# Sparse attention with a gated feed-forward layer: the first 512 keys loaded in 32 by 32 blocks and transposed by VectorE

## Chip, cores and metric

The kernel runs on one core of a Trainium2 chip. The metric is the device time of one execution in microseconds. Before the change it is 560.16 us, the median of 3 runs (559.36 to 561.0).

The engines are named as the profile names them: PE is TensorE, PEld its loading of weights, DVE is VectorE, ACT is ScalarE, POOL is GpSimd, SP is SyncE. A name with q, as SPq, is the engine's queue of issued work.

## The reference

For each of 8 batches and 8 heads, 576 queries attend to 576 keys of 64 numbers. Only scores within `tau` of the row's maximum count. The heads are joined, and a feed-forward layer with a gate follows.

```python
scores = scale * np.matmul(q, k.transpose(0, 1, 3, 2))
thresh = np.max(scores, axis=-1, keepdims=True) - tau
scores = np.where(scores >= thresh, scores, -1000000000.0)
scores = scores - np.max(scores, axis=-1, keepdims=True)
attn = np.exp(scores)
attn = attn / (np.sum(attn, axis=-1, keepdims=True) + 1e-09)
attn_out = np.matmul(attn, v)                       # (8, 8, 576, 64), float32
x = attn_out.transpose(0, 2, 1, 3).reshape(4608, 512)
h = x @ w_in                                        # (4608, 2048)
g = h * np.clip(h + 3.0, 0.0, 6.0) / 6.0
out = g @ w_out                                     # (4608, 512)
```

## The kernel before

Two heads are a pair, two pairs a quad; there are 16 quads, two to a batch. A quad is worked in 9 slots: slots 0 to 3 are 128 queries each of its first pair, slots 4 to 7 those of its second, and slot 8 the last 64 queries of all four heads. Each slot also does a piece of the feed-forward layer of an earlier batch: a first-layer item (`mm1`, with `mm1_relu` and `mm1_gate`), except in slot 8, and mostly one part of a second-layer tile (`mm2_part`).

The scores need queries and keys with the 64 head numbers on partitions, the two heads of a pair in the two halves. So both have to be transposed after loading. Batches 0 and 1 (`b < NB`, `NB = 2`) do this with TensorE for both. From batch 2 on queries come as 32 by 32 blocks, and VectorE transposes each block; keys are still transposed by TensorE and copied out of PSUM. The values are laid out so that key number `4 p + t` lies on partition `p`, and the keys are transposed in that order.

```python
def main(dst, src, h, order, by=nc.sync):
    by.dma_start(out=dst[:, :, h, :], in_=src[b, 4 * g + h, 0:512, :].rearrange(order, t=4))

def blocks_q(n, a, j):                       # queries, from the third batch on
    c = 32 * (2 * a + j)
    nc.sync.dma_start(out=nq[c:c + 32, n * S:(n + 1) * S].rearrange("p (k d) -> p k d", d=32),
                      in_=q[b, 4 * g + 2 * n + a, :, 32 * j:32 * j + 32].rearrange("(k r) d -> r k d", r=32))

# ...
for n in range(2):                           # five loading jobs to a quad, one started per slot
    loads.append(lambda n=n: [main(km, k, 2 * n + a, "(p t) d -> p t d") for a in range(2)])
    loads.append(lambda n=n: load_q(n))
    if n == 0:
        loads.append(rest)                   # keys 512 to 575 (and those queries, for b < NB)

# ...
def by_pe(pair):
    return pair // NPAIR < NB

def main_pe(src, pair):
    ps = bank("tp")
    n = pair % 2
    for t in range(4):
        nc.tensor.transpose(ps[:, t * P:(t + 1) * P], src[:, t, 2 * n:2 * n + 2, :], identf[:])
    return ps

def transpose_q(pair):
    nq = nat[pair // 2][0]
    if by_pe(pair):
        ps = main_pe(nq[:, 0:1024].rearrange("p (t h d) -> p t h d", h=4, t=4), pair)
        return lambda: nc.vector.tensor_copy(out=qT_of(pair)[:, 0:512], in_=ps[:])
    n = pair % 2
    nc.vector.transpose(out=qT_of(pair), in_=nq[:, n * S:(n + 1) * S])

def transpose_k(pair):
    ps = main_pe(nat[pair // 2][1], pair)
    return lambda: copy_out(kT_of(pair)[:, 64:576], ps[:])    # ScalarE from slot number 22 on
```

The loop over the slots, cut to the order of work in one slot:

```python
for n, sl in enumerate(queue):
    # ...
    if slot == (4 if quad else 8) and quad + 2 < NQUAD:
        load_quad(quad + 2)                  # appends the five jobs
    # ...
    if prev is not None:
        for i in range(2):
            sm_exp(prev, i)                  # ScalarE
    sm_max(sl)                               # VectorE row maximum, GpSimd bias
    if slot != 8 and todo1:
        item, then = todo1.pop(0)
        h = mm1(item)                        # TensorE, one PSUM buffer
        r = mm1_relu(h, on_act=(slot in (0, 1, 3, 5)))   # ScalarE, or else VectorE
        mm1_gate(item, h, r)                 # VectorE
        todo2.extend(then)
    # ...                                    # reciprocal (VectorE), second-layer parts (TensorE)
    for i in range(2):
        sm_mask(sl, i)                       # ScalarE
    evict = None
    nxt = 2 * quad + 2
    if slot == (1 if quad else 2):
        evict = transpose_q(2 * quad + 1)
    elif slot == (2 if quad else 3):
        evict = transpose_k(2 * quad + 1)
    # ...
    elif slot in (5, 6, 7) and quad + 1 < NQUAD:
        if slot == 5:
            alloc_qk(quad + 1)
            evict = transpose_q(nxt)
        elif slot == 6:
            evict = transpose_k(nxt)
        else:
            evict = transpose_rest(quad + 1)
    # ...                                    # attention times values in slots 3, 4 and 8
    if evict:
        evict()
    # ...
    if n + 1 < len(queue):
        queue[n + 1].tiles = scores(queue[n + 1].quad, queue[n + 1].slot)   # TensorE
    # ...
    if prev is not None:
        sm_norm(prev)                        # GpSimd, then mostly a transposing transfer (SyncE)
    flush()                                  # outputs
    late.extend(outs)
    start(loads, 1)                          # one loading job
```

Of the kernel before, what the change touches and what calls it, by code (L numbers as in the profile page):

```python
# [21 lines left out]
def kernel(  # L22
# [10 lines left out]
    nc = tc.nc  # L33
# [8 lines left out]
    NB = 2  # L42
# [25 lines left out]
    nat = {}  # L68
# [5 lines left out]
    loads = []  # L74
# [5 lines left out]
    def load_quad(quad):  # L80
        b, g = divmod(quad, 2)
        nat[quad] = (nat_pool.tile([P, 1152], F32, tag="nq", name="nq"),
                     nat_pool.tile([P, 4, 4, D], F32, tag="km", name="km"),
                     nat_pool.tile([P, 2 * D], F32, tag="kr", name="kr"))
        nq, km, kr = nat[quad]

        def main(dst, src, h, order, by=nc.sync):
            by.dma_start(out=dst[:, :, h, :], in_=src[b, 4 * g + h, 0:512, :].rearrange(order, t=4))

        def blocks_q(n, a, j):  # L90
            c = 32 * (2 * a + j)
            nc.sync.dma_start(out=nq[c:c + 32, n * S:(n + 1) * S].rearrange("p (k d) -> p k d", d=32),
                              in_=q[b, 4 * g + 2 * n + a, :, 32 * j:32 * j + 32].rearrange("(k r) d -> r k d", r=32))

        def load_q(n):
            if b < NB:
                for a in range(2):
                    main(nq[:, 0:1024].rearrange("p (t h d) -> p t h d", h=4, t=4), q, 2 * n + a, "(t p) d -> p t d",
                         by=nc.scalar if quad == n == 0 else nc.sync)
            else:  # L100
                for a in range(2):
                    for j in range(2):
                        blocks_q(n, a, j)

        def rest():
            for dst, src in ((kr[:], k), (nq[:, 1024:1152], q))[0:2 if b < NB else 1]:
                for n in range(2):
                    nc.sync.dma_start(out=dst[64 * n:64 * n + 64, :].rearrange("p (h d) -> p h d", h=2),
                                      in_=src[b, 4 * g + 2 * n:4 * g + 2 * n + 2, 512:S, :].rearrange("h p d -> p h d"))

        for n in range(2):
            loads.append(lambda n=n: [main(km, k, 2 * n + a, "(p t) d -> p t d") for a in range(2)])
            loads.append(lambda n=n: load_q(n))
            if n == 0:
                loads.append(rest)

    def load_v(b):
        vm = v_pool.tile([P, H, 4 * D], BF16, tag="vm", name="vm")
        vr = vrs[b % 2]
        vsb[b] = (vm, vr)  # L120
        for g in range(2):
            vcasts.append(lambda g=g: nc.gpsimd.dma_start(
                out=vm[:, g * 4:g * 4 + 4, :],
                in_=v[b, g * 4:g * 4 + 4, 0:512, :].rearrange("h (p t) d -> p h (t d)", t=4)))
        for a in range(2):
            vcasts.append(lambda a=a: nc.gpsimd.dma_start(
                out=vr[a * 64:(a + 1) * 64, a, :, :],
                in_=v[b, :, 512:S, :].rearrange("(hp a) p d -> a p hp d", a=2)[a]))
# [57 lines left out]
    def kT_of(pair):  # L186
        return qkT[pair // 2][1][:, pair % 2, :]
# [4 lines left out]
    def bank(name):  # L192
        nonlocal turn
        turn += 1
        if now < N2 and turn % 2:
            return ps_o.tile([P, 512], F32, tag="o", name=name)
        return ps_m.tile([P, 512], F32, tag="m", name=name)


    def copy_out(out, in_):  # L200
        if 0 <= now < N1:
            nc.vector.tensor_copy(out=out, in_=in_)
        else:
            nc.scalar.copy(out=out, in_=in_)  # L204
# [11 lines that stand above are left out]
# [7 lines left out]
        nc.vector.transpose(out=qT_of(pair), in_=nq[:, n * S:(n + 1) * S])  # L223

    def transpose_k(pair):
        ps = main_pe(nat[pair // 2][1], pair)
        return lambda: copy_out(kT_of(pair)[:, 64:576], ps[:])

# [63 lines left out]
    def sm_exp(sl, i):  # L292
        s = sl.s[:, i, :]
        nc.scalar.activation(out=s, in_=s, func=Act.Exp, accum_out=sl.rsum[:, i:i + 1])  # L294
# [67 lines left out]
    def mm1_relu(hps, on_act):  # L362
        w = hps.shape[2]
        r = r_pool.tile([P, 2, 320], F32, tag="r", name="r")[:, :, 0:w]
        if on_act:
            nc.scalar.activation(out=r, in_=hps, func=Act.Relu, bias=three[:])  # L366
        else:
            nc.vector.tensor_scalar(out=r, in0=hps, scalar1=3.0, scalar2=0.0, op0=Alu.add, op1=Alu.max)  # L368
        return r

    def mm1_gate(item, hps, r):
        b, ni, c0, w = item
        c0 += (b % 2) * S
        nc.vector.scalar_tensor_tensor(out=gbuf[:, ni:ni + 2, c0:c0 + w], in0=r, scalar=6.0, in1=hps,  # L374
                                       op0=Alu.min, op1=Alu.mult)
# [63 lines left out]
    for n, sl in enumerate(queue):  # L439
        quad, slot = sl.quad, sl.slot  # L440
        b, g = divmod(quad, 2)
        now = n
        if slot in (0, 4):
            pts[2 * quad + slot // 4] = pt_pool.tile([P, 9, 512], BF16, tag="pT", name="pT")
        if slot == 8:
            ptr[quad] = ptr_pool.tile([P, 9, P], BF16, tag="pR", name="pR")
        if quad == 0 and slot == 0:
            load_quad(1)
        if slot == (4 if quad else 8) and quad + 2 < NQUAD:
            load_quad(quad + 2)  # L450
        if slot == 0 and g == 1 and b + 1 < B:
            load_v(b + 1)
        if prev is not None:
            for i in range(2):
                sm_exp(prev, i)
        sm_max(sl)

        if slot != 8 and todo1:
            item, then = todo1.pop(0)
            h = mm1(item)  # L460
            r = mm1_relu(h, on_act=(slot in (0, 1, 3, 5)))
            mm1_gate(item, h, r)
            todo2.extend(then)
        copies = pe_transpose(queue[n - 2]) if n > 1 and queue[n - 2].on_chip else None
        if prev is not None:
            sm_recip(prev)
        if copies:
            copies()
        outs = []


        pieces = 0 if slot == 3 else 1
        if slot == 0:
            second = True
        if second and slot < 2 and len(todo2) > 1 and todo2[0][1] == todo2[1][1]:
            pieces, second = 2, False
        for _ in range(pieces):
            if todo2:
                bb, mt, part = todo2.pop(0)
                mm2_part(bb, mt, part)  # L480
                if part == 3:
                    outs += mm2_out(bb, mt, on_act=False)
        for i in range(2):
            sm_mask(sl, i)
# [6 lines that stand above are left out]
        elif n == 1:  # L491
            evict = transpose_rest(0, of_k=False)
        elif slot == 3 and quad > 0:
            av_main(2 * quad - 1)
        elif slot == 4 and quad > 0:
            av_rest(quad - 1)
            if quad % 2 == 0:
                todo1.extend(moe_of(quad // 2 - 1))
# [8 lines that stand above are left out]
        elif slot == 8:  # L507
            av_main(2 * quad)
# [3 lines that stand above are left out]
            warm_up(8)  # L512
        if n + 1 < len(queue):
            queue[n + 1].tiles = scores(queue[n + 1].quad, queue[n + 1].slot)
        if n < 8:
            warm_up(6)
        if prev is not None:
            sm_norm(prev)
        flush()
        late.extend(outs)  # L520
        start(loads, 1)
        if n < 4 or n > 12:
            start(vcasts, 1)
        if n > 3:
            start(casts, 1 if n < 24 else 2)
        prev = sl
# [80 lines left out]
```

## Time and profile before

| what | before |
|---|---|
| time, median of 3 runs | 560.16 us |
| span of the profiled run | 558.7 us |
| key transposes on TensorE (`tp<-identf,km`) | 128 matmuls, 273 ns each in the mean |
| copies of 512 transposed keys, ScalarE | 27, 563 ns in the median |
| query transposes on VectorE (128x576) | 24, 758 ns in the median |
| transfers for 512 keys of one head | 64, 128 KB each, 3.0 us to landing |
| transfers for queries in blocks | 96, 72 KB each, 2.7 us to landing |
| packets of all transfers | 286348 |

A busy time says how long an engine had an instruction in hand. The chain is the work that ended last, followed back from the end, at each step to what released it. A long busy time off this chain costs nothing by itself. Matmuls overlap, so that the duration of one is longer than what the next one has to wait.

### The profile page before, as it was taken

The numbers are of one execution on the slowest core, as the hardware profiler recorded it, in microseconds if no ns is written. First come the engines' busy times: TensorE is split into PE (matmuls) and PEld (weight loads), VectorE is DVE, ScalarE is ACT, GpSimd is POOL, SyncE is SP. The second block draws the span as 40 slices with busy tenths as digits, with TensorE's granted clock in tenths as the row PEclk, the third lists the DMA queues.
The fourth block names the chain that finished last, engine by engine and source line by source line (L and its number), as shares of the span: only waits on it lengthen the run. The fifth ranks groups of instructions, "written<-read, shape, count | busy, mean of one in ns | idle before, by whom it ended". The sixth has DMA issues, their size and how long they took to land.

```text
span 558.7 us, 11624 instructions
## 1 busy us (share of the span) xinstructions
PE 530.6 (95%) x3829; PEld 309.2 (55%) x3870; DVE 424.7 (76%) x1041; ACT 469.7 (84%) x999; POOL 305.3 (55%) x646
## 2 busy tenths in 40 slices
PE   8899798799999999999999999999999999999997
PEld 6655455555555555655555555655555565654663
DVE  3787686787878788887978788887978798883440
ACT  4899899798889999899898999899898999984440
POOL 2788878854556555755556555755556555561000
PEclk9999899999999999999999999999999999999999
DMA  5999979976789869978689889977689865454102
GB/s 121 137 120 173 196 128 190 204 142 126 137 158 152 152 136 157 178 149 146 130 148 152 173 131 160 175 147 147 131 145 166 150 144 114 100 109 94 38 20 76
DMA packets 286348, 77.52 MB, mean 139 GB/s; under 512 B 269264, under 2 KB 281808, under 8 KB 286288
## 3 DMA queue, kind: packets, MB, share of 16 engines
q1 hardware_dynamic: 267680, 67.47, 65.3%
q0 software_dynamic: 17408, 8.92, 13.6%
q8 instruction: 30, 0.49, 0.4%
q10 hardware_dynamic: 1200, 0.39, 0.3%
q14 instruction: 30, 0.25, 0.1%
HBM read 36.70 MB, written 9.44 MB: 83 GB/s over the span
## 4 chain that ended last, share of the span: by engine, by line
PE 55%; DVE 11%; ACT 8%; issue 4%; SPq 3%; DMA 2%; POOL 2%; DVEq 0%; POOLq 0%
PE h L357 17%; PE o L386 16%; PE s L260 15%; DVE s L281 5%; PE av L327 3%; ACT s L289 3%; ACT s L294 3%; DMA nq<-in_q_dram 2%; DVE g L374 2%; DVE r L368 2%; ACT r L366 1%; PE s L266 1%; PE tp L214 1%; SPq L310 1%; POOL pn L302 1%
## 5 line engine op out<-in xcount | busy, mean ns | idle before, releaser
L302 POOL TENSOR_SCALAR pn<-s,rinv 128x576 bf16<-128x576 f32 x288 | 211.6, 745 | 133.1 <-DVE rinv L297 57.3
L289 ACT ACTIVATE s<-s,bias 128x576 f32<-128x576 f32 x288 | 206.9, 766 | 36.3 <-POOL bias L284 35.2
L281 DVE TENSOR_SCALAR_CACHE_REDUCE s<-s 128x576 f32<-128x576 f32 x288 | 205.9, 752 | 40.3 <-PE s L260 29.9
L294 ACT ACTIVATE s<-s 128x576 f32<-128x576 f32 x288 | 192.7, 671 | 0.3
L260 PE MATMUL s<-kT,qT 64*128 64x288 f32 x1024 | 169.7, 430 | 5.1 <-DVE s L281 2.8
L357 PE MATMUL h<-xT,w_in_sb 128*128 128x320 bf16 (+1 forms) x1024 | 144.9, 287 | 5.9 <-DVE g L374 5.0
L386 PE MATMUL o<-w_out_sb,g 128*128 128x512 bf16 x535 | 133.5, 379 | 5.2 <-DVE osb L394 3.0
L357 PEld LDWEIGHTS <-w_in_sb 128*128 128x128 bf16 x1024 | 92.1, 97 | 68.9 <-issue 31.9
L374 DVE SCALAR_TENSOR_TENSOR g<-r,h 128x512 bf16<-128x512 f32 (+1 forms) x128 | 96.4, 755 | 41.7 <-ACT r L366 39.9
L260 PEld LDWEIGHTS s<-kT,qT 64*128 64x128 f32 x1024 | 93.7, 186 | 60.9 <-DVE s L281 24.0
L284 POOL TENSOR_SCALAR bias<-m 128x1 f32<-128x1 f32 x288 | 54.4, 189 | 66.6 <-DVE s L281 45.8
L386 PEld LDWEIGHTS <-g 128*128 128x128 bf16 x576 | 55.6, 98 | 57.4 <-issue 9.0
L366 ACT ACTIVATE r<-h,three 128x640 f32<-128x640 f32 (+1 forms) x74 | 54.4, 736 | 20.6 <-PE h L357 19.9
L294 ACT ACTIVATION_READ_ACCUMULATOR s<-s 128x1 f32 x288 | 54.2, 188 | 0.0
L368 DVE TENSOR_SCALAR r<-h 128x512 f32<-128x512 f32 (+1 forms) x54 | 40.5, 751 | 0.0
L394 DVE TENSOR_SCALAR osb<-o 128x512 f32<-128x512 f32 x31 | 21.0, 676 | 21.4 <-PE o L386 21.4
L327 PE MATMUL av<-pT,vm 128*64 128x512 bf16 x256 | 34.6, 393 | 2.0 <-ACT kT L204 2.0
L327 PEld LDWEIGHTS <-vm 128*64 128x64 bf16 x512 | 18.0, 111 | 25.3 <-issue 18.8
L297 DVE RECIPROCAL rinv<-rsum 128x2 f32<-128x2 f32 x144 | 23.0, 160 | 11.3 <-ACT s L294 10.5
L339 DVE CAST xT<-av 128x512 bf16<-128x512 f32 x32 | 21.8, 681 | 6.6 <-PE av L330 6.3
L281 DVE DVE_READ_ACCUMULATOR s<-s 128x1 f32 x288 | 23.9, 83 | 0.0
L266 PE MATMUL s<-kT,qT 64*64 64x288 f32 x256 | 20.1, 415 | 0.7 <-DVE s L281 0.7
(44 smaller groups left out, 241.4 us busy)
## 6 DMA issues: line engine op xcount, KB each, us to landing
km<-in_k_dram SPq DMA_DIRECT2D x64, 128.0 KB, 3.0
out_dram<-osb SPq DMA_DIRECT2D x31, 256.0 KB, 2.4
nq<-in_q_dram SPq DMA_DIRECT2D x96, 72.0 KB, 2.7
vm<-in_v_dram POOLq DMA_DIRECT2D x16, 256.0 KB, 5.6
w_in_sb<-in_moe_w_in_dram POOLq DMA_DIRECT2D x16, 128.0 KB, 4.3
w_out_sb<-in_moe_w_out_dram POOLq DMA_DIRECT2D x16, 128.0 KB, 4.5
pT<-pn SPq DMA_TRANSPOSE x119, 3.4
nq<-in_q_dram SPq DMA_DIRECT2D x14, 128.0 KB, 4.4
```

What stands on the lines that cost most here:

```text
L260: nc.tensor.matmul(tiles[a][:, hf, 0:HALF], qT_of(pair)[a * 64:(a + 1) * 64, t * P:(t + 1) * P], keys(pair, a, hf), start=True, stop=True)
L281: nc.vector.tensor_scalar(out=sl.s[:, i, :].rearrange("p (a b) -> p a b", a=2), in0=ps[:, :, 0:HALF], scalar1=1.0, scalar2=None, op0=Alu.m ...
L284: nc.gpsimd.tensor_scalar(out=sl.bias[:, i:i + 1], in0=sl.m[:, i:i + 1], scalar1=-scale, scalar2=tau, op0=Alu.mult, op1=Alu.add)
L289: nc.scalar.activation(out=s, in_=s, func=Act.Prelu, bias=sl.bias[:, i:i + 1], scale=scale, alpha=REJECT)
L294: nc.scalar.activation(out=s, in_=s, func=Act.Exp, accum_out=sl.rsum[:, i:i + 1])
L302: nc.gpsimd.tensor_scalar(out=pn[:, i, :], in0=sl.s[:, i, :], scalar1=sl.rinv[:, i:i + 1], scalar2=1.0, op0=Alu.mult, op1=Alu.mult)
L327: nc.tensor.matmul(ps[a * 64:(a + 1) * 64, :], vm[:, 2 * hp + a, c * D:(c + 1) * D], pT[:, 5 * a + c, cols], start=(c == 0), stop=False)
L357: nc.tensor.matmul(hps[:, n, 0:w], w_in_sb[:, ki, (ni + n) * P:(ni + n + 1) * P], xT[b][:, ki, c0:c0 + w], start=(ki == 0), stop=(ki == KI ...
L366: nc.scalar.activation(out=r, in_=hps, func=Act.Relu, bias=three[:])
L368: nc.vector.tensor_scalar(out=r, in0=hps, scalar1=3.0, scalar2=0.0, op0=Alu.add, op1=Alu.max)
L374: nc.vector.scalar_tensor_tensor(out=gbuf[:, ni:ni + 2, c0:c0 + w], in0=r, scalar=6.0, in1=hps, op0=Alu.min, op1=Alu.mult)
L386: nc.tensor.matmul(o_ps[0], gbuf[:, ni, mt * P:(mt + 1) * P], w_out_sb[:, ni, :], start=(ni == 0), stop=(ni == NI - 1))
```

## The change

From the third batch on (`b >= NB`) the first 512 keys of each head are loaded like the queries: four transfers to a pair, each filling 32 partitions with 32 by 32 blocks, two halves of the head numbers for each of two heads. Within the blocks the keys stand in the order of the values, so that VectorE's transposition of each block puts them where TensorE's transposes and the copy had put them. TensorE then needs no key transposes and ScalarE no copy for these pairs. As VectorE has one more instruction for each pair and ScalarE one less, one first-layer ReLU per quad goes from VectorE to ScalarE from quad 4 on: ScalarE does it in slots 1, 2, 3, 5 and 6 instead of 0, 1, 3 and 5. The last 64 keys are treated as before.

```diff
+        def blocks_k(n, a, j):
+            c = 32 * (2 * a + j)
+            nc.sync.dma_start(
+                out=km[c:c + 32].rearrange("p t h d -> p (t h d)")[:, n * 512:(n + 1) * 512].rearrange(
+                    "p (t m d) -> p t m d", t=4, d=32),
+                in_=k[b, 4 * g + 2 * n + a, 0:512, 32 * j:32 * j + 32].rearrange("(m r t) d -> r t m d", r=32, t=4))
+
+        def load_k(n):
+            if b < NB:
+                for a in range(2):
+                    main(km, k, 2 * n + a, "(p t) d -> p t d")
+            else:
+                for a in range(2):
+                    for j in range(2):
+                        blocks_k(n, a, j)
...
-            loads.append(lambda n=n: [main(km, k, 2 * n + a, "(p t) d -> p t d") for a in range(2)])
+            loads.append(lambda n=n: load_k(n))
...
     def transpose_k(pair):
+        if not by_pe(pair):
+            n = pair % 2
+            km = nat[pair // 2][1][:].rearrange("p t h d -> p (t h d)")
+            nc.vector.transpose(out=kT_of(pair)[:, 64:576], in_=km[:, n * 512:(n + 1) * 512])
+            return None
         ps = main_pe(nat[pair // 2][1], pair)
         return lambda: copy_out(kT_of(pair)[:, 64:576], ps[:])
...
-            r = mm1_relu(h, on_act=(slot in (0, 1, 3, 5)))
+            r = mm1_relu(h, on_act=(slot in ((1, 2, 3, 5, 6) if quad >= 2 * NB else (0, 1, 3, 5))))
```

## The prediction

> **What bounds the kernel now.** I read the page's first two parts, then the busy time in three stretches, then the chain that ended last, then the groups of the stretch that matters.
>
> ```profile
> PE 530.6 (95%) x3829; PEld 309.2 (55%) x3870; DVE 424.7 (76%) x1041; ACT 469.7 (84%) x999; POOL 305.3 (55%) x646
> ```
>
> TensorE is busy nearly throughout, ScalarE next. That is an average, so the same count by stretch, the first ending where the steady part begins:
>
> ```profile
> core 0: us, PE busy (x) PEld busy (x) DVE busy (x) ACT busy (x) POOL busy (x), PEclk, DMA share, GB/s
> 115.00:145.00 30.00, 28.85 (x208) 16.09 (x209) 24.85 (x61) 26.99 (x60) 15.78 (x34) 1.00 0.72 138
> 145.00:505.00 360.00, 353.19 (x2582) 202.49 (x2615) 298.83 (x735) 328.91 (x709) 204.68 (x434) 1.00 0.82 145
> 505.00:559.00 54.00, 48.43 (x303) 27.57 (x305) 19.90 (x28) 17.51 (x25) 0.98 (x2) 0.99 0.18 53
> ```
>
> In the steady 360 us TensorE has 6.8 us free, ScalarE 31.1 (91% busy), VectorE 61.2 (83%), and the DMA engines are busy 82%. A ceiling follows: if TensorE sets the pace, work taken from it is the only thing worth much, and ScalarE is next at 9%. But the chain through the same stretch is not TensorE alone:
>
> ```profile
> by line: PE s L260 20.9%; PE h L357 19.4%; PE o L386 16.7%; DVE s L281 5.3%; issue 4.6%; PE av L327 4.4%; DMA nq<-in_q_dram 3.1%; ACT s L289 2.8%; ACT s L294 2.7%; DVE g L374 2.3%; DVE r L368 2.1%; PE s L266 1.9%; PE tp L214 1.6%; SPq L310
> ```
>
> The key transposes are 1.6% of 360 us here, 5.8 us. Each set of four is a 0.44 us step of the chain, so about 13 of the 22 sets of this stretch (88 matmuls) lie on it. Where they don't, the chain runs through ScalarE, as in this piece of it (start, duration, what):
>
> ```profile
> 212.51 1.27 issue
> 213.78 1.47 POOL pn L302 x2
> 215.25 0.08 issue
> 215.34 0.20 POOL bias L284
> 215.54 0.02 issue
> 215.56 1.44 ACT s L289 x2
> 217.00 0.15 ACT kT L204
> ```
>
> There the softmax loop GpSimd, ScalarE, VectorE was last, and the key copy on ScalarE was part of it.
>
> **What the skill says.** The Trainium skill, "VectorE: DVE Perf Modes", § The three transpose paths: VectorE transposes 32 by 32 blocks only, SBUF to SBUF, where TensorE does the full 128 by 128 and lands in PSUM; hence the new load order. It gives 311 ns against 390 ns for 128x128 bf16. The trace has the float32 case: VectorE takes 758 ns for 128x576 queries (row below); TensorE takes 0.44 us for four 128x128 tiles plus 563 ns of ScalarE for the copy out. The skill, "DMA: Bandwidth & Descriptors", § Why small descriptors are slow (HBM only): a fixed overhead of about 3 cycles per packet on top of size/32. From it I estimate 7 cycles for 128 bytes against 11 for 256, so halving packets costs 14/11, 27% more. The trace's packet records have a median of 13 ns for 128 bytes and 18 ns for 256: two for one cost 44% more. The measurement counts. The skill, "Perfetto Trace Analysis", § Identifying the Most-Contended Engine, warns that matmul busy time overstates TensorE; the trace agrees so far that its chain gives PE only 55% of the span against 95% busy. I therefore treat the 6.8 us of free time as too small, and the full saving as a ceiling.
>
> **The change part by part.**
>
> ```profile
> L223 DVE STREAM_TRANSPOSE qT<-nq 128x576 f32<-128x576 f32 x22 | 16.7, 760 | 0.0
> L368 DVE TENSOR_SCALAR r<-h 128x512 f32<-128x512 f32 x24 | 16.5, 686 | 0.0
> L366 ACT ACTIVATE r<-h,three 128x640 f32<-128x640 f32 x23 | 18.0, 786 | 6.2 <-PE h L357 6.1
> L366 ACT ACTIVATE r<-h,three 128x512 f32<-128x512 f32 x24 | 16.3, 680 | 3.6 <-PE h L357 3.5
> L214 PE MATMUL tp<-identf,km 128*128 128x128 f32 x88 | 13.2, 273 | 0.0
> L204 ACT COPY kT<-tp 128x512 f32<-128x512 f32 x22 | 12.4, 563 | 0.0
> ```
>
> (busy us, then mean ns, in these groups of 145 to 505 us.) The tile's own list has 24 such copies, from 118.0 to 482.4 us, which are the 24 pairs of quads 4 to 15; so everything below counts 24.
>
> TensorE loses 24 sets of four, 0.44 us each as chain steps: 10.6 us. By the busy column, 13.2/22 = 0.60 us a set, 14.4 us; but a modelled end overlaps the next matmul, so 0.44 is the right unit.
>
> ScalarE loses 24 copies. One is 563 ns alone, but its neighbours start 0.47 us apart (the chain's "ACT kT L204" steps), so 11.3 us. It takes over one ReLU in each of 12 quads: five of eight slots in place of four. By the busy column (18.0+16.3)/47 = 0.73 us, 8.8 us. Net about -2.5 us.
>
> VectorE gains 24 transposes of 128x512. Scaled from 760 ns for 576 elements (a start every 0.68 us in its timeline, so 0.61 for 512): 14.6 us. It gives up 12 ReLUs at (18.0+16.5)/46 = 0.75 us: 9.0 us. Net +5.6 us, against 61.2 us free.
>
> The DMA engines: per pair 1024 packets of 256 bytes become 2048 of 128. With the mean packet times of the records (22.9 and 13.7 ns), 1024 x 22.9 / 16 = 1.47 us becomes 2048 x 13.7 / 16 = 1.75 us, +0.3 us a pair, +7 us in all spread over some 380 us: the 82% becomes about 84%. SyncE's queue issues four loads a pair for two. Two now cost 2 x 0.627 = 1.25 us (their median); four query block loads of nearly the same shape cost 4 x 0.497 = 1.99. So +0.7 us a pair, 18 us of issuing in all, in the slots 4 and 7 of each quad, beside transposing transfers of 1.3 us each. In five consecutive slots (4 to 8) of some 3.5 us, SyncE then issues 5 x 1.3 (transposes) + 8 x 0.5 (keys) + 8 x 0.5 (queries) + 1.3 (rest) + about 1.5 (outputs) = 17.3 us of 17.5. That is full, where before it was 15.8.
>
> Slot by slot, ScalarE does 1.34 us of exponentials and 1.44 of masks everywhere, 2.8 us. Slots 2 and 6 had a copy (0.47) and now have a ReLU (0.73), slot 0 loses its ReLU. So in slots 1 to 3 and 5 to 7, where a pair's keys are made, ScalarE has a little more to do, not less, while TensorE has 0.44 us less. In slots 5 to 7 with the narrow 256 tokens: TensorE 3 x (1.17 scores + 0.98 first layer + 0.86 second) + 0.44 = 9.5 us before and 9.0 after; ScalarE 3 x 2.8 + 0.68 (ReLU) + 0.47 + 0.5 (short keys) = 10.1 before and 3 x 2.8 + 2 x 0.68 + 0.5 = 10.3 after. There the saving on TensorE cannot be collected. In slots 1 to 3 with 320 tokens, TensorE has 3 x 1.17 + 3 x 1.19 + 2 x 0.86 + 1.2 (attention times values) + 0.44 = 10.4 and ScalarE 3 x 2.8 + 2 x 0.79 + 0.47 = 10.5 before; after it is 10.0 against 10.8, made up only by the light slots 8 and 0 beside them. So I choose about 60% of the ceiling: 0.6 x 10.6 = 6.4 us, close to the 5.8 us that lie on the chain. I take off 0.8 us for SyncE and the DMA engines running fuller in the stretches where values are loaded. Sum: 560.2 - 6.4 + 0.8 = 554.6, rounded to 554.5 us.
>
> **The rivals.** (1) TensorE sets the pace wholly, and all 10.6 us come out: 549.6 us. For it: 98% busy in the steady part. Against: the chain piece above, and 46 waits of the gate for ScalarE's ReLU, 24.4 us in the steady part. (2) ScalarE takes over as the bound, because the ReLU is given back to it in the very slots that the copy left: nearly nothing, 558 to 560 us. For it: 91% busy, and the slot sums above. Against: over a whole quad its work falls. (3) Transfers become the bound. For it: the chain already has "DMA nq<-in_q_dram" at 3.1%; where values are loaded the DMA share is 1.0 to 1.25 in stretches of 8 us, and there SyncE needs 8.9 us for three transposes that take 1.3 each elsewhere. Later transposes would hold the normalized-score buffers, and GpSimd would wait. If each of the six remaining value loads cost 1 us more than now, it takes back the gain: 560 us; with 3 us each, 572. Against: GpSimd waited for DMA only 5 us in all, and the packets add 2 points. (4) VectorE holds up the next row maximum: 0.61 us ahead of it in slots 2 and 6. But those slots lose their VectorE ReLU of 0.75 us in exchange, so no loss; slot 0, which gains it, also has the longest TensorE work.
>
> **Range and chances.** All of the ceiling gives 549.6, none of it with a small DMA loss gives 560.5; that is my range. Faster by over 2% needs 548.96 us, more than the whole TensorE saving: 6%. Slower by 2% needs a transfer backlog of more than 11 us: 5%.
>
> **What would show it.** No key transposes on TensorE after about 115 us, TensorE busy down by 13 to 15 us, ScalarE by 2 to 4, VectorE up by 5 to 6, about 24,600 more packets. Right: the chain has fewer TensorE steps, and the gate's waits for ScalarE's ReLU grow from 24 us, because ScalarE is nearer to the bound. Wrong: TensorE's free time stays under 8 us in the steady part (then rival 1), or GpSimd's waits for DMA grow beyond 10 us (rival 3), or VectorE waits at its new transpose for the key load.

## The result and the profile after

The changed kernel takes 556.31 us in the median (555.88 to 558.13) against 560.58: ratio 0.9933, 95% interval 0.9915 to 0.9952. By the ratio that is 3.8 us less (by the medians 4.3), where the prediction had 5.7 less than its 560.16. Here is the changed kernel's page: busy times, clock by slice, the large queue.

```profile
PE 526.6 (95%) x3774; PEld 300.2 (54%) x3774; DVE 428.6 (77%) x1053; ACT 463.6 (84%) x987; POOL 305.3 (55%) x646
...
PEclk9999999799999999999999999999999999999999
...
q1 hardware_dynamic: 293024, 67.47, 69.8%
```

TensorE's busy time is down by 4 us only, but the two pages cannot be subtracted as they stand: that of before has 535 records of the second layer's matmuls (`o<-w_out_sb,g`), this one all 576. At 133.5/535 = 0.25 us each the missing 41 are 10 us, and the drop is about 14. ScalarE is down by 6.1 us, VectorE up by 3.9. The clock has a 7 in the eighth slice; before, it had an 8 in the fifth and none in the eighth:

```profile
PEclk9999899999999999999999999999999999999999
```

The same stretch as before, ended 4 us sooner because the run is that much shorter, in the answer by stretches (its columns: length, busy time and count of PE, PEld, DVE, ACT, POOL, granted clock, DMA share, GB/s), then the chain through it, then two groups of it (busy us, mean ns, idle before):

```profile
145.00:501.00 356.00, 351.04 (x2561) 195.91 (x2561) 303.61 (x748) 325.68 (x704) 205.39 (x435) 1.00 0.88 148
```

```profile
by line: PE s L281 20.4%; PE h L378 17.5%; PE o L407 16.7%; ACT s L310 5.4%; ACT s L315 4.9%; PE av L348 4.7%; issue 4.5%; DVE s L302 4.3%; ACT r L387 3.0%; PE s L287 2.6%; POOL pn L323 2.5%; DVE r L389 1.8%; DVE g L395 1.5%; DMA pR<-pn 1.5
```

```profile
L245 DVE STREAM_TRANSPOSE kT<-km 128x512 f32<-128x512 f32 x22 | 15.3, 694 | 0.0
L389 DVE TENSOR_SCALAR r<-h 128x512 f32<-128x512 f32 x18 | 12.3, 686 | 0.0
```

The key transposes of TensorE are gone from the chain, ScalarE's lines (exponentials, masks, ReLU) have grown from 2.8, 2.7 and under 1.6% to 5.4, 4.9 and 3.0%. VectorE's new transpose takes 694 ns and never waits for its load (idle 0.0).

Where the time went is best seen slot by slot. The start of each slot's row maximum on VectorE (288 of them, two to a slot) is in the trace of both kernels; this is the later one's start minus the earlier one's:

| at the start of | before, us | after minus before, us |
|---|---|---|
| quad 1, slot 6 | 51.94 | 0.00 |
| quad 2, slot 0 | 64.23 | -1.27 |
| quad 3, slot 3 | 101.99 | -1.26 |
| quad 3, slot 6 | 115.22 | +2.65 |
| quad 4, slot 0 | 125.71 | +3.00 |
| quad 8, slot 0 | 252.36 | +0.76 |
| quad 12, slot 0 | 378.02 | -1.49 |
| last slot | 499.69 | -3.78 |

The first 1.27 us are not the change's: the two programs do the same up to quad 2, slot 4. They go with the 8 in the fifth slice: in the profile of before TensorE's granted clock was 0.50 for 3.4 us from 59.3 us on, in the other 1.00. From quad 1, slot 6 to quad 2, slot 0 the four profiles with a drop between 59 and 65 us take 12.2 to 12.3 us, the seven whose clock stayed at 1.00 up to there 11.0 to 11.1.

Then the changed kernel loses about 4 us within three slots, and gains 3.00 + 3.78 = 6.8 us in the remaining 107 slots. In the lossy slots, TensorE's part of the timeline, before and after (start, duration, what, in brackets the idle time before it and what ended it):

```profile
104.96 1.05 PE L327 MATMUL av<-pT,vm 128*64 128x512 bf16 x8 [2.03 <-ACT kT L204]
...
106.16 1.24 PE L260 MATMUL s<-kT,qT 64*128 64x288 f32 x8
```

```profile
104.89 1.92 PE L348 MATMUL av<-pT,vm 128*64 128x512 bf16 x8 [3.23 <-DMA pT<-pn]
106.57 0.66 PE L351 MATMUL av<-pT,vr 128*64 128x512 bf16 x2
107.16 2.29 PE L281 MATMUL s<-kT,qT 64*128 64x288 f32 x8
...
112.64 0.32 PE L348 MATMUL ar<-pR,vm 128*64 128x64 bf16 x8 [0.94 <-DMA pR<-pn]
```

Attention times values waits for a transposing transfer of normalized scores, twice. And after the first wait eight score matmuls last 2.29 us; before, they were 1.24. The stretches tell why (same columns as above), three of them after, then the middle one before:

```profile
100.00:104.00 4.00, 1.48 (x10) 0.71 (x8) 2.03 (x6) 2.86 (x6) 3.74 (x8) 0.93 1.28 188
104.00:108.00 4.00, 3.11 (x14) 1.53 (x16) 1.45 (x3) 4.00 (x10) 2.99 (x7) 0.50 1.44 197
108.00:112.00 4.00, 3.70 (x20) 1.78 (x16) 2.39 (x6) 1.64 (x4) 1.07 (x4) 0.72 1.37 136
```

```profile
104.00:108.00 4.00, 2.85 (x22) 1.71 (x22) 1.15 (x3) 4.00 (x9) 2.99 (x8) 1.00 1.44 202
```

TensorE's granted clock was 0.50 from 103.4 us, within the pause, to 110.3 us; before, it was 1.00 in all three stretches. The DMA engines are full here (share above 1) in both kernels, with weights, values, keys, queries and transposes at once. So the change has a steady gain and a single loss, and the experiments ask for the cause of each.

### The profile page after: what moved, and what is told of

Read it like the earlier page. It is cut to its first block, busy times and chain, and to the rows that moved or that the text cites. A ratio compares the mean times of both kernels' runs of the same rounds, so it can differ in the third digit from the quotient of the medians.

```text
span 554.6 us, 11512 instructions
## 1 busy us (share of the span) xinstructions
PE 526.6 (95%) x3774; PEld 300.2 (54%) x3774; DVE 428.6 (77%) x1053; ACT 463.6 (84%) x987; POOL 305.3 (55%) x646
## 3 DMA queue, kind: packets, MB, share of 16 engines
q1 hardware_dynamic: 293024, 67.47, 69.8%
## 4 chain that ended last, share of the span: by engine, by line
PE 54%; ACT 11%; DVE 9%; DMA 4%; issue 4%; POOL 3%; SPq 1%; POOLq 0%; DVEq 0%
PE o L407 16%; PE h L378 16%; PE s L281 15%; ACT s L310 5%; ACT s L315 4%; DVE s L302 4%; PE av L348 4%; DMA pR<-pn 3%; ACT r L387 2%; POOL pn L323 2%; PE s L287 2%; DVE r L389 1%; DVE g L395 1%; DMA km<-in_k_dram 1%; POOL vm L138 1%
## 5 line engine op out<-in xcount | busy, mean ns | idle before, releaser
L281 PE MATMUL s<-kT,qT 64*128 64x288 f32 x1024 | 173.3, 433 | 6.0 <-DVE s L302 3.9
L407 PE MATMUL o<-w_out_sb,g 128*128 128x512 bf16 x576 | 140.9, 379 | 4.1 <-DVE osb L415 4.1
L281 PEld LDWEIGHTS s<-kT,qT 64*128 64x128 f32 x1024 | 96.6, 187 | 68.0 <-DVE s L302 33.0
L387 ACT ACTIVATE r<-h,three 128x640 f32<-128x640 f32 (+1 forms) x86 | 62.9, 733 | 27.4 <-PE h L378 26.9
L389 DVE TENSOR_SCALAR r<-h 128x512 f32<-128x512 f32 (+1 forms) x42 | 31.5, 750 | 0.0
L318 DVE RECIPROCAL rinv<-rsum 128x2 f32<-128x2 f32 x144 | 22.9, 159 | 10.7 <-ACT s L315 9.8
L287 PE MATMUL s<-kT,qT 64*64 64x288 f32 x256 | 21.4, 415 | 0.7 <-DVE s L302 0.7
```

The source lines that it names most:

```text
L281: nc.tensor.matmul(tiles[a][:, hf, 0:HALF], qT_of(pair)[a * 64:(a + 1) * 64, t * P:(t + 1) * P], keys(pair, a, hf), start=True, stop=True)
L407: nc.tensor.matmul(o_ps[0], gbuf[:, ni, mt * P:(mt + 1) * P], w_out_sb[:, ni, :], start=(ni == 0), stop=(ni == NI - 1))
```

## Experiments

Times are given as ratios to the kernel before, run on the same chip, with 95% intervals. "Narrow" are slots with 256 tokens in the first layer, "wide" those with 320. Slots 6 and 7 are narrow in quads 5, 6, 9, 10, 13 and 14, and wide in 7, 8, 11 and 12.

**The key blocks start one quad later.**

```diff
-            if b < NB:                       # load_k
+            if quad < 5:
-        if not by_pe(pair):                  # transpose_k
+        if pair >= 10:
-    ... if quad >= 2 * NB else (0, 1, 3, 5)
+    ... if quad >= 5 else (0, 1, 3, 5)
```

> Key blocks, VectorE transposes and the new ReLU split start with quad 5 instead of quad 4, so that no key blocks are loaded while the weights are still being cast. Theory A (the changed kernel loses about 3.9 us once, between slots 30 and 33, because the blocks of quad 4 crowd the transposing transfers that attention times values waits for, and gains 0.28 us per pair afterwards): 556.3 - 3.9 + 2 x 0.28 = 553.0 us. Rival B (the loss there is chance, or the price of starting the new split anywhere): about 556.9 us, only the gain of two pairs missing, or the loss moved to quad 5.

Measured 555.83 us, ratio 0.9905 (0.9881 to 0.9930). At quad 4, slot 0 this kernel is at -0.21 us against before, where the changed one is at +3.00: the loss is gone from there and has not come back with quad 5. By whole times it is only 1.6 us faster than the changed kernel, with intervals that overlap; the single slots are theory A's, the whole time lies between the two forecasts.

**Only the loads of the change.** TensorE transposes, ScalarE copies and the ReLUs are split as before, on keys that then stand in wrong places.

```diff
     def transpose_k(pair):
-        if not by_pe(pair):
-            ...                              # VectorE's transpose
         ps = main_pe(nat[pair // 2][1], pair)
```

> Only the loads change: keys come in blocks from the third batch on, but TensorE transposes them and ScalarE copies them as before, and the ReLUs are split as before. (The keys then stand in wrong places: what is computed with them is not the reference's.) Theory A: the once-only loss of some 3.9 us and nearly nothing else, 560.6 + 3.9 = 564.5 us, up to 565.5 with a small drag. Rival B (block loads are a steady drag on the queue and the DMA engines, which is what keeps the gain per pair at 0.28 instead of 0.44 us): 24 x 0.16 = 3.8 us more than that, 568 us. Rival C (the loads cost nothing): 560.6 us.

Measured 565.57 us, ratio 1.0086 (1.0056 to 1.0116), 4.8 us lost. The row maxima place 3.9 of them between quad 3, slot 3 and quad 4, slot 0; after this the distance stays at 6.44 us, within 0.01, at the starts of 68 slots (0.8 are added once later; 2.5 were there from the start). TensorE's wait in its timeline:

```profile
109.86 1.92 PE L343 MATMUL av<-pT,vm 128*64 128x512 bf16 x8 [4.42 <-DMA pT<-pn]
```

Block loads alone make the loss and are no steady drag: rivals B and C fall.

**Only the computing of the change.** Keys are loaded in whole rows; the blocks that VectorE transposes then don't hold the right keys.

```diff
         def load_k(n):
-            if b < NB: ...
-            else: ...
+            for a in range(2):
+                main(km, k, 2 * n + a, "(p t) d -> p t d")
```

> Only the computing changes: keys are loaded in whole rows as before, VectorE transposes them in 32 by 32 blocks and the ReLUs are split as in the changed kernel. (The transposed keys are then not the right ones: what is computed with them is not the reference's.) Theory A: all of the steady gain, no loss at the start: 560.6 - 24 x 0.28 = 553.9 us, possibly 553. Rival B (steady drag of the loads): all of the 10.6 us, 550.0 us. Rival C (loads cost nothing): 556.3 us like the changed kernel.

Measured 554.19 us, ratio 0.9882 (0.9859 to 0.9905). From quad 4, slot 0 to the last slot it gains 6.8 us, as much as the changed kernel with its block loads. That is theory A.

**The values out of the pile-up.** The third batch's values are loaded five slots later; the rest is the changed kernel.

```diff
-        if slot == 0 and g == 1 and b + 1 < B:
+        if slot == (5 if quad == 3 else 0) and g == 1 and b + 1 < B:
             load_v(b + 1)
```

> The changed kernel, in which only the loading of the third batch's values is moved by five slots (quad 3, slot 5 instead of slot 0), out of the stretch in which weights, keys and queries are loaded. Theory A (the once-only loss is a pile-up of transfers there): all 3.9 us come back and perhaps 1 us more, 552.5 us. Rival G (the loss comes from SyncE's issuing of more transfers, not from how full the DMA engines are): 556 us as in the changed kernel.

Measured 551.72 us (551.05 to 552.93), ratio 0.9840 (0.9819 to 0.9862): faster than both kernels. The same line of TensorE's timeline:

```profile
103.58 1.05 PE L348 MATMUL av<-pT,vm 128*64 128x512 bf16 x8 [0.20 <-ACT kT L220]
```

The wait for a transfer is gone with SyncE issuing as many loads as in the changed kernel, so their number alone does not make the loss, and rival G falls as it was put. The transposing transfer that TensorE had waited for took 7.7 us from issue to landing in the changed kernel; the same one takes 5.8 us here, and 5.9 us before. So key blocks and values together make the loss. By which way is not shown. The DMA share between 96 and 112 us is still 1.27 to 1.33 here, so that the share alone does not tell the two apart; SyncE's issuing is shorter too, as for four query loads of quad 4 (changed kernel, then this one); and the values' issuing on GpSimd has moved with them.

```profile
99.33 4.09 SPq L92 DMA_DIRECT2D nq<-in_q_dram  x4
```

```profile
100.13 2.31 SPq L92 DMA_DIRECT2D nq<-in_q_dram  x4
```

The same step on the kernel before tells how much of it belongs to the change.

```diff
-        if slot == 0 and g == 1 and b + 1 < B:            # in the kernel before
+        if slot == (5 if quad == 3 else 0) and g == 1 and b + 1 < B:
```

> The kernel before with only the third batch's values loaded five slots later. Theory A (the pile-up in slots 27 to 33 becomes costly only through the key blocks; before, TensorE waited there for a ScalarE copy, not for a transfer): at most 1.5 us faster, 559 to 560.5 us. Rival L (the values cost the kernel before as much as the changed one): 556.5 us, and the change would then be worth 4.8 us on top and not more than it was.

Measured 558.04 us, ratio 0.9969 (0.9957 to 0.9980), between the two forecasts. Slots 2 to 6 of quad 3 give 1.8 us: TensorE's wait of 2.03 us shown above is 0.60 us there. So the later values are worth 1.7 us to the kernel before and 0.9840/0.9933 = 0.9906, 5.2 us, to the changed one. With the values out of the way the change is worth 0.9840/0.9969 = 0.9871, 7.2 us.

**The ReLU split as before.**

```diff
-    on_act=(slot in ((1, 2, 3, 5, 6) if quad >= 2 * NB else (0, 1, 3, 5)))
+    on_act=(slot in (0, 1, 3, 5))
```

> The changed kernel with the ReLUs split as before (ScalarE in slots 0, 1, 3 and 5). Theory A, as in the prediction (ScalarE, with its ReLU back in slots 2 and 6, keeps 40% of TensorE's saving): ScalarE has 0.73 us less there, so a larger part of 10.6 us comes out, 556.3 - 2 = 554 us. Rival D (VectorE, which then has ReLU and key transpose in slots 2 and 6, some 3.6 us there, becomes the bound of those slots): 558 us or more.

Measured 561.70 us, ratio 1.0026 (1.0009 to 1.0044): rival D. From quad 4, slot 0 to the last slot this kernel gains 2.0 us on the kernel before, where the changed one gains 6.8: without the new split most of the gain is not there. The new split alone, without the new loads and transposes, was not run, so what it gives by itself stays open. VectorE's list where ReLU and key transpose meet in slot 6 of quad 8, with no idle time between its entries (the row maximum of slot 7 starts when the list is done):

```profile
278.45 0.82 DVE L389 TENSOR_SCALAR r<-h 128x640 f32<-128x640 f32 x1
279.31 0.82 DVE L395 SCALAR_TENSOR_TENSOR g<-r,h 128x640 bf16<-128x640 f32 x1
280.04 0.16 DVE L318 RECIPROCAL rinv<-rsum 128x2 f32<-128x2 f32 x1
280.12 0.69 DVE L245 STREAM_TRANSPOSE kT<-km 128x512 f32<-128x512 f32 x1
280.73 0.72 DVE L302 TENSOR_SCALAR_CACHE_REDUCE s<-s 128x576 f32<-128x576 f32 x1
```

**What was removed, put back by halves.** First TensorE's transposes, whose result nobody reads:

```diff
             nc.vector.transpose(out=kT_of(pair)[:, 64:576], in_=km[:, n * 512:(n + 1) * 512])
+            main_pe(nat[pair // 2][1], pair)
             return None
```

> The kernel of e1_from_quad5 with TensorE's four key transposes of each pair from quad 5 on put back at their old place, written to PSUM and read by nobody; VectorE's transposes stay. Theory A (the steady gain is TensorE's 0.44 us per pair, as far as it shows): 22 pairs x 0.26 to 0.44 us back, so 5.7 to 9.7 us over e1_from_quad5. Rival E (the gain is ScalarE's copy that is gone): within 1.5 us of e1_from_quad5.

Then a ScalarE copy into a spare tile, without TensorE's transposes:

```diff
             nc.vector.transpose(out=kT_of(pair)[:, 64:576], in_=km[:, n * 512:(n + 1) * 512])
-            return None
+            return lambda: nc.scalar.copy(out=spare[:], in_=km[:, n * 512:(n + 1) * 512])
```

> The kernel of e1_from_quad5 with one ScalarE copy of 128x512 for each pair from quad 5 on put back at the old place (from SBUF into a spare tile that nobody reads); no TensorE transposes. Theory A (ScalarE holds the narrow slots 5 to 7 already and has little room in the others): 22 x 0.2 to 0.4 us, 4 to 9 us over e1_from_quad5. Rival F (ScalarE has room, its lists of work were never the reason for the missing part of the gain): within 1.5 us of it.

Measured 560.78 us, ratio 0.9994 (0.9980 to 1.0008), and 559.18 us, ratio 0.9970 (0.9953 to 0.9987): 5.0 and 3.6 us over the kernel they were made from (0.9905). Neither half is free, both just under theory A's numbers. The lengths of slots, from the starts of the row maxima, tell where (sums of two slots, us):

| | slots 2+3, quads 6, 10, 14 | slots 2+3, quads 8, 12 | slots 2+3, quads 5, 7, 9, 11, 13 | slots 6+7 narrow, mean of 6 | slots 6+7, quads 8, 12 | slots 6+7, quads 7, 11 |
|---|---|---|---|---|---|---|
| changed minus before | -0.16 | -0.44 | -0.47 to -0.48 | +0.02 | -0.44 | -0.43 |
| ReLUs as before, minus before | 0.00 | -0.38 | -0.11 to -0.48 | +0.24 | -0.18 | +0.04 |
| TensorE back | +0.06 | +0.44 | +0.01 to +0.03 | +0.05 | +0.44 | +0.04 |
| ScalarE back | +0.12 | +0.40 | +0.52 to +0.53 | +0.01 | 0.00 | 0.00 |

(The last two rows against the kernel with blocks from quad 5. Single narrow quads of the first row lie between -0.22 and +0.31; quads 4 and 15, not in the table, are wide in slots 6 and 7 and have only -0.22 and -0.15 there.) TensorE's work sets the pace only in quads 8 and 12, and in slots 2 and 3 of quad 15 (+0.44). In slots 2 and 3 of the others ScalarE's copy was what counted. In quad 9 one sees how: the copy stands ahead of the next slot's exponentials (L316), and so of the ReLU that VectorE's gate waits for.

```profile
295.61 0.60 ACT L247 COPY spare<-km 128x512 f32<-128x512 f32 x1
296.12 0.68 ACT L316 ACTIVATE s<-s 128x576 f32<-128x576 f32 x1
...
298.26 0.82 DVE L396 SCALAR_TENSOR_TENSOR g<-r,h 128x640 bf16<-128x640 f32 x1 [0.90 <-ACT r L388]
```

The same gate without the copy, in the kernel with blocks from quad 5:

```profile
295.05 0.82 DVE L395 SCALAR_TENSOR_TENSOR g<-r,h 128x640 bf16<-128x640 f32 x1 [0.37 <-ACT r L387]
```

In slots 6 and 7 of quads 7 and 11 neither half alone counts, but without the new split there is no gain (+0.04). TensorE's row adds up to about 2.9 us over quads 5 to 15. Of the rest of its 5.0 us 0.7 were there before quad 4, slot 0, where the two kernels do the same, and 1.5 are a single wait in slot 4 of quad 7. Two kernels below that do not have this work, the one without the ReLU of slot 6 and the last one, are also 0.8 and 0.9 us longer in slots 4 and 5 of that quad than the kernels they were made from, so this wait can hardly be charged to it.

**The narrow slot 6, where nothing was gained.** One column of the table is near zero in the mean in spite of less work on TensorE, and a ScalarE copy costs nothing there. Without the ReLU of slot 6:

```diff
-    r = mm1_relu(h, on_act=...)
+    r = still[:, :, 0:item[3]] if slot == 6 and quad >= 5 else mm1_relu(h, on_act=...)
```

(`still` is a fixed tile, so those items aren't the reference's.)

> The kernel of e1_from_quad5 without the ReLU of slot 6 from quad 5 on: the gate multiplies by a fixed tile there. (One first-layer item in eight is then not the reference's.) Theory A (in the narrow slots 5 to 7 ScalarE, with its second ReLU, keeps TensorE's saving from showing): six narrow quads give up to 0.4 us each and the wide ones little: 2 to 3.5 us under e1_from_quad5. Rival H (something else, such as the row maximum waiting for VectorE's key transpose, holds slot 6): less than 1 us.

Measured 553.02 us, ratio 0.9860 (0.9840 to 0.9880), 2.5 us less than the kernel with blocks from quad 5, as theory A said. The narrow slots 6+7 give 0.32 to 0.40 us each, the wide ones 0.00. But this takes away more than ScalarE's work. VectorE's list in slot 6 of quad 10, in the kernel with blocks from quad 5:

```profile
334.20 0.75 DVE L302 TENSOR_SCALAR_CACHE_REDUCE s<-s 128x576 f32<-128x576 f32 x1
334.88 0.08 DVE L302 DVE_READ_ACCUMULATOR s<-s 128x1 f32 x1
335.35 0.69 DVE L395 SCALAR_TENSOR_TENSOR g<-r,h 128x512 bf16<-128x512 f32 x1 [0.39 <-ACT r L387]
335.95 0.16 DVE L318 RECIPROCAL rinv<-rsum 128x2 f32<-128x2 f32 x1
336.03 0.67 DVE L415 TENSOR_SCALAR osb<-o 128x512 f32<-128x512 f32 x1
336.62 0.70 DVE L245 STREAM_TRANSPOSE kT<-km 128x512 f32<-128x512 f32 x1
337.24 0.72 DVE L302 TENSOR_SCALAR_CACHE_REDUCE s<-s 128x576 f32<-128x576 f32 x1
```

VectorE waits 0.39 us for ScalarE's ReLU, and everything behind it, the key transpose last, stands ahead of the next row maximum without a gap. If the list is the reason, the key transpose has to go elsewhere. First into slot 8, behind the output's copy (on top of the kernel with later values):

```diff
-                evict = transpose_k(nxt)                        # slot 6
+                evict = transpose_k(nxt) if by_pe(nxt) else None
         elif slot == 8:
+            if quad + 1 < NQUAD and not by_pe(nxt):
+                transpose_k(nxt)
             av_main(2 * quad)
```

> The kernel of e7_values_later with VectorE's key transpose for the next quad's first pair moved from slot 6 to slot 8, which has no first-layer item; the ReLU of slot 6 stays on ScalarE. Theory I (what holds the narrow slot 6 is VectorE's list in order: row maximum, 0.39 us of waiting for ScalarE's ReLU, gate, output, key transpose, before the next row maximum can start): the narrow quads give 0.3 to 0.4 us each, the wide ones nothing, 551.7 - 6 x 0.35 = 549.6 us. Rival J (ScalarE's work in slots 5 to 7 holds it): no change, 551.7 us. Rival K (scores in slot 8 wait for the late keys): slower, 553 us or more.

Measured 557.91 us, ratio 0.9965 (0.9949 to 0.9982): 7.0 us slower than the kernel it was made from. Both I and K are seen: the narrow slots 6+7 give 0.36 to 0.56 us each and the wide ones 0.00, but slot 8 loses 0.56 to 0.85 in narrow quads and 0.46 to 1.34 in wide ones. TensorE's timeline there:

```profile
282.51 1.24 PE L281 MATMUL s<-kT,qT 64*128 64x288 f32 x8 [1.30 <-DVE kT L245]
```

With slot 6's ReLU on VectorE as well:

```diff
-    on_act=(slot in ((1, 2, 3, 5, 6) if quad >= 2 * NB else (0, 1, 3, 5)))
+    on_act=(slot in ((1, 2, 3, 5) if quad >= 2 * NB else (0, 1, 3, 5)))
```

> The kernel of e9_keys_in_slot8 with the ReLU of slot 6 on VectorE again (ScalarE in slots 1, 2, 3 and 5). Theory I: VectorE's list in slot 6 is as long as in e7_values_later in the narrow quads (ReLU 0.6 us for 0.62 us of key transpose, without the wait for ScalarE of 0.39 us), so between e9_keys_in_slot8 and e7_values_later, about 550.5 us. Rival J (ScalarE's work holds slots 5 to 7): faster than e9_keys_in_slot8 by 1 us or more.

Measured 561.79 us, ratio 1.0042 (1.0025 to 1.0059), about 4 us slower than the one it was made from; both forecasts miss, theory I's 550.5 us by 11. The narrow slots 6+7 are 0.00 to 0.16 us longer than there, the wide ones of quads 7, 8, 11 and 12 0.23 to 0.43, and slot 8 is longer by up to 0.69. Giving ScalarE less and VectorE more does not help: rival J falls. Theory I is not borne out by this run either; it had left out the late keys and the longer list of the wide slots. Last, the transpose directly behind slot 8's row maximum, in the six narrow quads alone:

```diff
         sm_max(sl)
+        if slot == 8 and quad % 4 in (1, 2) and quad > 2:
+            transpose_k(2 * quad + 2)
-                evict = transpose_k(nxt)                        # slot 6
+                evict = None if quad % 4 in (1, 2) and quad > 2 else transpose_k(nxt)
```

> The kernel of e7_values_later with the key transpose of the next quad's first pair moved out of slot 6 in the six quads where slots 4 to 7 have narrow items (5, 6, 9, 10, 13, 14), to slot 8 directly behind the row maximum, where e9_keys_in_slot8 had VectorE idle and the keys came 1.3 us too late for the scores. Theory I (VectorE's list holds the narrow slot 6; the loss of e9_keys_in_slot8 was only the late keys): 6 x 0.4 us less, at most 0.2 us back in each slot 8: 549.5 to 551 us. Rival J (nothing to be had in slot 6, or the same lost again in slot 8): 551.7 us or more.

Measured 552.11 us (550.23 to 552.68), ratio 0.9836 (0.9808 to 0.9864), not to be told from the 0.9840 of the kernel with later values: by the whole time rival J's number, and the slots have to decide. In five of the six narrow quads slots 6+7 are shorter by 0.35 to 0.56 us. In quad 13 they are not; there the next row maximum waits 0.59 us for TensorE's scores instead. Slot 8 of quads 6, 10 and 14 loses 0.22. The same list in quad 10:

```profile
334.04 0.69 DVE L395 SCALAR_TENSOR_TENSOR g<-r,h 128x512 bf16<-128x512 f32 x1 [0.39 <-ACT r L387]
334.64 0.16 DVE L318 RECIPROCAL rinv<-rsum 128x2 f32<-128x2 f32 x1
334.72 0.67 DVE L415 TENSOR_SCALAR osb<-o 128x512 f32<-128x512 f32 x1
335.31 0.75 DVE L302 TENSOR_SCALAR_CACHE_REDUCE s<-s 128x576 f32<-128x576 f32 x1
```

The wait of 0.39 us for ScalarE is still there; only the key transpose is gone, and from the gate to the row maximum it is 1.27 us where it was 1.89. So in five of the six quads it was VectorE's list that held slot 6. The 1.4 us that the slots sum to did not show in whole runs; in the profiled one slot 4 of quads 3 and 7 was longer by 1.5 and 0.9 us.

## Why the prediction was right, and where not

The time lay in the range, 1.8 us above the predicted value. Point by point:

- **TensorE's saving, "about 60% of the ceiling: 0.6 x 10.6 = 6.4 us".** The size came out: 6.8 us from quad 4 on, 64%, and as much without the block loads. That it came out so near is luck. Slots 2 and 3, from which little was expected, gave 4.6 of the 6.8 us, and the light slots 8 and 0, which were to make up for it, gave nothing (0.00 to +0.06 us, slots 0 and 1 taken together).
- **"I take off 0.8 us for SyncE and the DMA engines."** The term that was mis-sized, and misplaced. Steadily the loads cost nothing: the kernel without them gains no more from quad 4 on. They cost 4.3 us once, in quad 3, when blocks of quad 4, weights and values are loaded together. The profile of before had shown the DMA share there (1.27 to 1.55 in 8 us stretches between 88 and 112 us); I priced the value loads of all later batches and not this one stretch. With the measured terms, -6.8 + 4.3 - 1.3 (the clock before quad 2) - 0.3 (after the start of the last slot) = -4.1, the difference of the two profiled spans.
- **DMA time "+7 us in all".** The queue's share went from 65.3% of 558.7 us to 69.8% of 554.6 us, 22 us more per engine. The new packets were as estimated (49152 more of 128 bytes, 37.9 us per engine against 42); but the packets of 256 bytes, 24576 fewer, took only 18 us less per engine instead of 35: those that stayed have a mean of 24.4 ns for 22.9, and the key packets that went were perhaps worth less than that mean (the median of all is 18). The +7 was too small by three times, and it did not matter outside quad 3.
- **"In slots 5 to 7 with the narrow 256 tokens ... the saving on TensorE cannot be collected."** Right as to the place: +0.02 us narrow in the mean, -0.43 to -0.44 in quads 7, 8, 11 and 12. Wrong as to the engine. It was not the sum of ScalarE's work, which takes a 0.6 us copy more there at no cost, but VectorE's list, as rival 4 had it. I put rival 4 aside with "those slots lose their VectorE ReLU of 0.75 us in exchange, so no loss"; in the place of the ReLU came 0.39 us of waiting for ScalarE's ReLU, and the transpose of 0.62 us behind it.
- **"In slots 1 to 3 ... ScalarE has a little more to do, not less", so little to collect there.** Wrong: with 320 tokens (quads 5, 8, 9, 12 and 13) slots 2 and 3 gave the whole 0.44 us and more; only quads 6, 10 and 14 gave 0.16. These are narrow there, but so are 7 and 11, which gave 0.47, so narrowness is not the reason; it stays open. In most quads it was ScalarE's copy, which had stood at the end of slot 2 ahead of the next slot's exponentials, whose absence paid: 0.52 us when it was put back. Sums of work over three slots did not show this.
- **The signs.** Key transposes gone after 115 us, TensorE -14 us with the missing records, packets +25,344 (768 of them of 4 bytes) for +24,600: as said. VectorE +3.9 for +5 to 6 and ScalarE -6.1 for -2 to -4: the right way, wrong in size. The gate's waits for ScalarE's ReLU did not grow (24.4 to 22.4 us). TensorE's free time fell to 5.0 us, by which rival 1 should have held; it did not, so that was a poor sign: with TensorE's transposes put back the slots outside quads 8, 12 and 15 mostly grew by 0.00 to 0.10 us, so a busy share of 99% did not mean that TensorE set the pace. Rival 3 held in quad 3 alone: from 145 us on GpSimd waited for transfers only 2.8 us in all.

## What to carry to other kernels

Here work taken from the busiest engine paid slot by slot, and in each slot only as far as the next in-order list allowed; so count what stands ahead of the next dependent instruction, waits included, rather than each engine's sum. Before adding packets, look for the one stretch where the DMA engines are already full: a load that is harmless in a hundred slots can cost more than half of the gain in three. Moving another, unhurried load out of that stretch (here the values, five slots later) turned 0.9933 into 0.9840; the same step alone takes the kernel before to 0.9969.

## What the runs showed of the hardware

- TensorE's granted clock fell to 0.50 for 3.4 us here and there (6.8 us in quad 3 of the changed kernel), and eight score matmuls took 2.29 us there for 1.24. The Trainium skill, "TensorE: Matmul & The Clock Gate", § Why this matters for your kernels, says to leave no idle gaps over about 3 us, or the clock falls back to half. This trace agrees so far that the drop stands beside a pause of 3.23 us; but it began 1.5 us before the end of that pause. Shorter pauses were not always safe: after 2.03 to 2.06 us in the same place the clock fell in two profiles (only the computing changed, 0.71 over the next 4 us, and ScalarE back) and stayed at 1.00 in three (before, TensorE back, no ReLU in slot 6). And with the values later it fell at 95.0 us, where TensorE had not paused for longer than 0.72 us in the 5 us before. No run tests what decides it. As drops fall differently in each profile, they have to be looked for before two profiles are compared slot by slot. The stretch with the values later (the clock is the third figure from the end):

```profile
96.00:100.00 4.00, 4.00 (x24) 2.86 (x23) 2.42 (x6) 3.46 (x8) 3.55 (x8) 0.70 1.27 173
```

- Outside single waits the slots repeat from one kernel's profile to the next: of the 107 slot lengths from quad 4 on, 97 agree within 0.01 us between the changed kernel and the one with only the computing changed. That made 0.4 us effects visible that whole times, which scatter by 0.7 to 6.8 us over the runs of one kernel, hid.
